# Linear attention, a dense MLP and a Sinkhorn mixture of experts in one kernel: every engine takes its instructions in the order of the source

## The chip, the cores and the metric

The kernel runs on one core of a Trainium2 chip. The engines named below are TensorE (PE, with its weight loads PEld), VectorE (DVE), ScalarE (ACT), GpSimd (POOL) and SyncE (SP, which issues the DMAs). The metric is the device time of one execution in microseconds (us), as the median of several runs.

## The reference

Three layers follow each other. The input of the first is q, k, v of 4 x 8 x 576 x 64; the two others work on 2304 tokens of 512 features, all in float32.

```python
# linear attention: softmax of q over its features, of k over the sequence
kv = np.einsum('bhsd,bhse->bhde', k_s, v)
x = np.einsum('bhsd,bhde->bhse', q_s, kv)          # -> 2304 x 512
# dense MLP, d_ff 2048
h = x @ w_in
x = np.maximum(0.01 * h, h) @ w_out
# mixture of 8 experts (512 -> 1024 -> 512), gates balanced by Sinkhorn
P = np.exp(x @ w_gate - (x @ w_gate).max())
for _ in range(8):
    P /= P.sum(1, keepdims=True) + 1e-09
    P /= P.sum(0, keepdims=True) + 1e-09
    P *= N / E
for e in range(E):
    out += P[:, e:e + 1] * (np.maximum(x @ w1[e], 0.0) @ w2[e])
```

## The kernel before

**Precision.** A float32 operand is split in two parts, hi (a rounded cast, on ACT) and lo (the remainder, on DVE or POOL), and each product is three matmuls: hi times hi, hi times lo, lo times hi.

**The dense MLP** runs in 96 steps: four phases of weights, in each six blocks of 384 tokens, in each four weight units. `first(s)` (twelve matmuls into a tile `ph`) gives the hidden tile: ACT writes `hh` hi and `g`, DVE writes `hh` lo from them (L188 to L190). `second(s)` (twelve matmuls into `y0` to `y3`) adds the hidden tile's share to the output, which at the end of four units goes to `acc` (L209 on ACT in phase 0, L211 on DVE later). A step is issued as two half-steps, and `first` runs one or two steps ahead of `second`.

**What is laid around the steps.** A table of half-steps (`at`, `plan`, `half_step`) says where other work is issued: `k_task` and `q_task` (attention of the next blocks, in phase 0), `prep_half(u, half)` (the conversion of half a weight unit: ACT L134, DVE L136, L137, L140, ACT L144, DVE L145, L146, POOL L148, L149, then the DMA of another half), the gates (`pg`) and, in phase 3, the first pairs of expert weights. Units 4 to 7 (phase 1) are converted at half-steps 35 to 47, units 8 to 11 from half-step 51 on and units 12 to 15 from 99 on, one half every 4.5 half-steps.

**The mixture** runs in 96 groups, 32 for each superblock of 768 tokens. `group(i)` has seven half-steps: t0 to t3 hold seven products of six matmuls (banks `pa` to `pd`; sums `c1`, `c2` on DVE, their hidden values in `xs`), t4 to t6 three output tiles `e` of twelve matmuls for the pair of groups before. Beside them a group converts the next group's weights: `wa<-pair`, `wa<-s` and `wb_t<-pair` (ACT L397, DVE L398), and DVE adds each `e` to `acc` (L491). `pre` is empty in groups 0 and 1, so the source has no `e` there. `balance` (the Sinkhorn iterations, matmuls `pmx`, `pmb`, `pcs0` to `pcs7`) is issued from group 0 on. `x_sums(sb)` makes the seven sums B11 to T4 of a superblock's input (four subtractions at L429, seven splits at L397/L398 into `xs`); for the second and third superblock it is issued from half-step t3 of groups 31 and 63, one piece per half-step.

**Who sets the order.** The source is written to the tile framework, which inserts the semaphores. Before the change its scheduler also orders each engine's instructions: by readiness and priority, so that an instruction whose inputs are there can be put ahead of others written earlier. An engine works through its own list from top to bottom.

## Time and profile before

| what | value |
|---|---|
| median of 3 runs | 2077.51 us (2077.18 to 2080.61) |
| the profiled execution | 2077.42 us, of which 2075.6 us lie in the span from the first to the last instruction |
| busy over the span | PE 98%, DVE 63%, ACT 38%, POOL 24% |
| mean granted clock of PE | 0.987 |
| the chain that ended last | PE 86%, DVE 6%, issue 5%, ACT 1%, DMA 1%, POOL 1% |

The shares are means over stages with different limits. The span falls into the dense MLP with the attention (0 to 554.8 us), the head of the mixture with the Sinkhorn iterations (554.8 to 619.4 us), and the rest of the mixture. In the windows PE busy below the window's length is time that PE stood still, and a PEclk below 1.00 is time at the lower of two clock levels.

### The profile page before, as it was taken

To read this page: it belongs to the slowest core of one execution; us is meant where nothing else is said; L and a number is where in the kernel's file an instruction comes from. 1 tells how busy PE (TensorE), PEld (TensorE's weight loads), DVE (VectorE), ACT (ScalarE), POOL (GpSimd) and SP (SyncE) were. 2 spreads that over 40 slices of the span, in tenths; PEclk is the share of its full clock that TensorE was granted. 3 is DMA by queue.
4 is the path that set the end of the run, shared out by engine and by line. 5 is a ranking of instruction groups with operands and counts; after the bars stand their busy time and mean duration, and the time that the engine had idled before them with its cause. 6 is when DMAs were issued, how large, how long until landed. Compare 5 with 4: busy or idle time off the path is not lost.

```text
span 2075.6 us, 26519 instructions
## 1 busy us (share of the span) xinstructions
PE 2024.7 (98%) x10447; PEld 1850.2 (89%) x10447; DVE 1303.4 (63%) x1899; ACT 794.1 (38%) x1342; POOL 508.3 (24%) x492
## 2 busy tenths in 40 slices
PE   7898798999999999999999999999999999999999
PEld 6898798999988988988988898898888889889887
DVE  8826826234486666666675666666676666666664
ACT  6644322223343343333344333343344433333431
POOL 5604404001121222222222212212212222222220
PEclk9999899999999999999999999999999999999999
DMA  6402202000121221221221211211213212212210
GB/s 239 151 7 74 89 3 89 1 1 1 42 81 41 82 82 41 82 82 41 82 97 57 81 64 59 82 56 67 82 41 112 81 41 81 82 41 82 82 41 31
DMA packets 65453, 138.57 MB, mean 67 GB/s; under 512 B 4656, under 2 KB 4656, under 8 KB 65328
## 3 DMA queue, kind: packets, MB, share of 16 engines
q1 hardware_dynamic: 65328, 136.87, 19.3%
q8 instruction: 82, 1.34, 0.3%
q14 instruction: 43, 0.35, 0.0%
HBM read 132.14 MB, written 4.72 MB: 66 GB/s over the span
## 4 chain that ended last, share of the span: by engine, by line
PE 86%; DVE 6%; issue 5%; ACT 1%; DMA 1%; POOL 1%; SPq 0%; POOLq 0%; ACTq 0%; DVEq 0%
PE e L172 38%; PE pa L172 9%; PE pc L172 9%; PE pd L172 9%; PE y L172 7%; PE ph L172 6%; PE pb L172 5%; DVE ca L140 1%; DVE ca L136 1%; DVE hh L190 1%; PE pg L172 1%; PE px L172 1%; DVE ca L137 1%; DVE raw L146 1%; PE pkv L172 1%
## 5 line engine op out<-in xcount | busy, mean ns | idle before, releaser
L172 PE MATMUL e<-wb_t,xs 128*128 128x512 f32 x3456 | 823.0, 395 | 0.2 <-DVE xs L498 0.2
L172 PEld LDWEIGHTS e<-wb_t,xs 128*128 128x128 f32 x3456 | 647.0, 188 | 149.6 <-DVE xs L498 0.7
L404 POOL TENSOR_TENSOR s<-pair 128x256 f32<-128x256 f32 x96 | 74.3, 774 | 1276.3 <-DMA pair<-in_w 703.8
L491 DVE SCALAR_TENSOR_TENSOR acc<-e,pm,acc 128x512 f32<-128x512 f32 x264 | 193.3, 745 | 104.9 <-PE e L172 102.3
L498 DVE SCALAR_TENSOR_TENSOR xs<-c,xs 128x384 fp32r<-128x384 f32 (+1 forms) x192 | 185.0, 982 | 84.2 <-ACT xs L497 81.1
L172 PE MATMUL pa<-xs,wa 128*128 128x384 f32 x1152 | 231.3, 335 | 2.2 <-ACT c L523 2.2
L172 PE MATMUL pc<-xs,wa 128*128 128x384 f32 x1152 | 230.8, 334 | 0.0
L172 PE MATMUL pd<-xs,wa 128*128 128x384 f32 x1152 | 230.6, 334 | 0.0
L497 ACT ACTIVATE xs<-c 128x768 fp32r<-128x768 f32 x192 | 126.6, 681 | 235.3 <-PE e L172 214.7
L172 PEld LDWEIGHTS pa<-xs,wa 128*128 128x128 f32 x1152 | 203.4, 188 | 11.5 <-ACT c L523 3.1
L172 PEld LDWEIGHTS pd<-xs,wa 128*128 128x128 f32 x1152 | 202.4, 188 | 0.0
L172 PEld LDWEIGHTS pc<-xs,wa 128*128 128x128 f32 x1152 | 202.3, 188 | 0.0
L190 DVE TENSOR_TENSOR hh<-g,hh 128x384 fp32r<-128x384 f32 x96 | 68.3, 712 | 187.6 <-ACT g L189 187.5
L398 DVE TENSOR_TENSOR wa<-s,wa 128x768 fp32r<-128x768 f32 x96 | 91.9, 957 | 105.0 <-ACT wa L397 102.8
L397 ACT CAST wa<-s 128x768 fp32r<-128x768 f32 x96 | 80.1, 835 | 174.4 <-POOL s L407 150.6
L513 DVE TENSOR_TENSOR c<-c 128x384 f32<-128x384 f32 x96 | 53.9, 562 | 135.3 <-ACT c L533 135.3
L172 PE MATMUL y<-hh,wa 128*128 128x384 f32 x576 | 119.8, 358 | 15.8 <-DVE acc L211 5.4
L172 PE MATMUL y<-hh,wb_t 128*128 128x384 f32 x576 | 118.6, 356 | 13.8 <-DVE hh L190 5.1
L523 ACT COPY c<-pa 128x384 f32<-128x384 f32 x96 | 46.2, 481 | 215.5 <-PE pa L172 164.9
L172 PEld LDWEIGHTS y<-hh,wa 128*128 128x128 f32 x576 | 108.0, 200 | 18.7 <-DVE hh L190 6.2
L172 PEld LDWEIGHTS y<-hh,wb_t 128*128 128x128 f32 x576 | 108.4, 202 | 16.6 <-DVE hh L190 6.4
L398 DVE TENSOR_TENSOR wa<-pair,wa 128x1024 fp32r<-128x1024 f32 x96 | 119.6, 1246 | 3.2 <-PE y L172 2.8
(106 smaller groups left out, 2515.5 us busy)
## 6 DMA issues: line engine op xcount, KB each, us to landing
pair<-in_w SPq DMA_DIRECT2D x192, 512.0 KB, 4.9
raw<-in_wm SPq DMA_DIRECT2D x32, 512.0 KB, 3.8
v<-in_vt SPq DMA_DIRECT2D x16, 320.0 KB, 4.7
k<-in_kt SPq DMA_DIRECT2D x16, 288.0 KB, 4.2
out<-acc SPq DMA_DIRECT2D x18, 256.0 KB, 2.0
acc<-in_q SPq DMA_DIRECT2D x5, 768.0 KB, 5.9
acc<-in_q SPq DMA_DIRECT2D x3, 256.0 KB, 5.2
wg_t<-in_wg SPq DMA_DIRECT2D x1, 16.0 KB, 8.9
```

What stands on the lines that cost most here:

```text
L136: nc.vector.tensor_scalar(af, af, EXP_MIN, EXP_MAX, op0=ALU.max, op1=ALU.min)
L137: nc.vector.tensor_scalar(a, a, 3, 0x3FFFFFFF, op0=ALU.logical_shift_left, op1=ALU.bitwise_and)
L172: nc.tensor.matmul(o, a, b, start=start, stop=stop, **more)
L190: nc.vector.tensor_tensor(hh[:, 1, :], g, r32(hh[:, 0, :]), op=ALU.subtract)
L397: nc.scalar.copy(hi, a)
L398: return lambda: nc.vector.tensor_tensor(lo, a, r32(hi), op=ALU.subtract)
L404: nc.gpsimd.tensor_tensor(s[:, 0], a21, a22, op=ALU.add)
L491: nc.vector.scalar_tensor_tensor(a, y, scale, a, op0=ALU.mult, op1=ALU.add)
L497: nc.scalar.activation(o[:, 0], p, AF.Relu)
L498: nc.vector.scalar_tensor_tensor(o[:, 1], p, 0.0, r32(o[:, 0]), op0=ALU.max, op1=ALU.subtract)
L513: add = lambda o, x, y: nc.vector.tensor_tensor(o, x, y, op=ALU.add)
L523: nc.scalar.copy(c1, bk[0])
```

## The change

The kernel enters a manual schedule: every engine's list is the order in which the source issues the instructions. With it the temporary `t1` of `x_sums` takes another buffer for the second and third superblock: tag `hh` of the pool `h` (two buffers, shared with `hh` and `c2`) in place of tag `s` (one buffer, shared with the sums of `pair_sums`).

```diff
@@ -68,6 +68,8 @@
     US = 4 * DM
     HX = KC // 2 * BLK
 
+
+    ctx.enter_context(tc.manual_schedule())
     const = ctx.enter_context(tc.tile_pool(name="const", bufs=1))
@@ -423,7 +425,8 @@
         b11, b12, b21, b22 = b
-        t1 = later["mo"].tile([P, KC // 2, BLK], F32, tag="s", name=f"t1_{sb}", bufs=1)
+        pool, tag, bufs = (hp_, "hh", 2) if sb else (later["mo"], "s", 1)
+        t1 = pool.tile([P, KC // 2, BLK], F32, tag=tag, name=f"t1_{sb}", bufs=bufs)
```

No instruction of the computation is added or taken away; lists change. Line numbers of the kernel after are higher by 2, and by 3 behind the second edit. Three places follow.

VectorE in phase 0, around steps 24 to 27 (`hhN` is the lo part of step N's hidden tile; `caU_H` and `rawU_H` are the conversion of half H of unit U; units 8 and 9 are needed in phase 2, from step 48 on). Before:

```order
L190 TENSOR_TENSOR hh23_1868<-g23_1869,hh23_1868 128x384
L146 SCALAR_TENSOR_TENSOR raw8_0_1941<-raw8_0_1941 128x512
L136 TENSOR_SCALAR ca9_0_2123<-ca9_0_2123 128x512
L137 TENSOR_SCALAR ca9_0_2123<-ca9_0_2123 128x512
L140 SCALAR_TENSOR_TENSOR ca9_0_2123<-raw9_0_1987,ca9_0_2123 128x512
L145 TENSOR_SCALAR raw9_0_1987<-ca9_0_2123 128x512
L146 SCALAR_TENSOR_TENSOR raw9_0_1987<-raw9_0_1987 128x512
L190 TENSOR_TENSOR hh24_1913<-g24_1914,hh24_1913 128x384
```

After, the same engine, four steps later in the program:

```order
L192 TENSOR_TENSOR hh26_2007<-g26_2008,hh26_2007 128x384
L147 TENSOR_SCALAR raw7_1_1922<-ca7_1_1969 128x512
L148 SCALAR_TENSOR_TENSOR raw7_1_1922<-raw7_1_1922 128x512
L192 TENSOR_TENSOR hh27_2048<-g27_2049,hh27_2048 128x384
L138 TENSOR_SCALAR ca8_0_2053<-ca8_0_2053 128x512
L139 TENSOR_SCALAR ca8_0_2053<-ca8_0_2053 128x512
L142 SCALAR_TENSOR_TENSOR ca8_0_2053<-raw8_0_1943,ca8_0_2053 128x512
L192 TENSOR_TENSOR hh28_2083<-g28_2084,hh28_2083 128x384
L147 TENSOR_SCALAR raw8_0_1943<-ca8_0_2053 128x512
L148 SCALAR_TENSOR_TENSOR raw8_0_1943<-raw8_0_1943 128x512
L192 TENSOR_TENSOR hh29_2120<-g29_2121,hh29_2120 128x384
```

The conversion of unit 8, which stood ahead of `hh24` before, now begins behind `hh27`, and one such half stands between several steps' hidden tiles; that of unit 9 comes later still.

TensorE at the Sinkhorn iterations (`pcsN` is the matmul of iteration N, `pX_1` are products of group 1, `e0_N` output tiles of groups 0 and 1). Before:

```order
L172 MATMUL pcs1_4740<-cs1_4698,ones_71 128x8
L172 MATMUL pd_1_4667<-xs_81,wa_82 128x384 x6
L172 MATMUL e0_0_4891<-wb_t_1680,xs_81 128x512 x2
L172 MATMUL e0_1_4907<-wb_t_1680,xs_81 128x512 x5
L172 MATMUL e0_0_4891<-wb_t_1680,xs_81 128x512 x2
L172 MATMUL e0_1_4907<-wb_t_1680,xs_81 128x512 x2
L172 MATMUL e0_0_4891<-wb_t_1680,xs_81 128x512
L172 MATMUL e0_1_4907<-wb_t_1680,xs_81 128x512 x2
L172 MATMUL e0_2_4935<-wb_t_1680,xs_81 128x512 x11
L172 MATMUL pcs2_4765<-cs2_4747,ones_71 128x8
L172 MATMUL e0_3_5028<-wb_t_1680,xs_81 128x512 x10
L172 MATMUL pcs3_4779<-cs3_4772,ones_71 128x8
```

After:

```order
L326 MATMUL pmx_4649<-ident_72,mrow_93 1x128
L174 MATMUL pmb_4654<-mall_94,ones_73 128x1
L174 MATMUL pa_1_4666<-xs_83,wa_84 128x384 x6
L174 MATMUL pb_1_4667<-xs_83,wa_84 128x384 x6
L174 MATMUL pcs0_4693<-cs0_4660,ones_73 128x8
L174 MATMUL pc_1_4668<-xs_83,wa_84 128x384 x6
L174 MATMUL pd_1_4669<-xs_83,wa_84 128x384 x6
L174 MATMUL pa_1_4666<-xs_83,wa_84 128x384 x6
L174 MATMUL pc_1_4668<-xs_83,wa_84 128x384 x6
L174 MATMUL pcs1_4742<-cs1_4700,ones_73 128x8
L174 MATMUL pd_1_4669<-xs_83,wa_84 128x384 x6
L174 MATMUL pcs2_4767<-cs2_4749,ones_73 128x8
```

The `e0` matmuls that stood between `pcs1`, `pcs2` and `pcs3` are gone from here (they now start in group 2, behind `pcs5`), and so are those between `pmx` and `pmb`; the next row after is `pcs3`.

VectorE at the boundary of superblocks in group 31 (`t1_1`, `acc2`, `acc3` belong to `x_sums(1)`, `xs` from them are its splits, `wa<-pair32` and `wa<-s32` the weights of the next group, L429 and L398 of before are L432 and L400 after). Before:

```order
L429 TENSOR_TENSOR t1_1_8328<-acc3_78,acc2_77 128x768
L398 TENSOR_TENSOR wa_82<-pair32_8207,wa_82 128x1024
L491 SCALAR_TENSOR_TENSOR acc0_75<-e14_1_8236,pm_74,acc0_75 128x512
L429 TENSOR_TENSOR acc3_78<-acc3_78 128x768
L491 SCALAR_TENSOR_TENSOR acc0_75<-e14_2_8251,pm_74,acc0_75 128x512
L513 TENSOR_TENSOR c1_31_8270<-pb_31_8266,c1_31_8270 128x384
L398 TENSOR_TENSOR xs_81<-acc2_77,xs_81 128x768
L398 TENSOR_TENSOR xs_81<-t1_1_8328,xs_81 128x768
L513 TENSOR_TENSOR c2_31_8269<-c2_31_8269 128x384
L398 TENSOR_TENSOR xs_81<-acc3_78,xs_81 128x768
L513 TENSOR_TENSOR c2_31_8269<-c2_31_8269,c1_31_8270 128x384
L498 SCALAR_TENSOR_TENSOR xs_81<-pa_31_8265,xs_81 128x384
```

After:

```order
L432 TENSOR_TENSOR t1_1_8330<-acc3_80,acc2_79 128x768
L432 TENSOR_TENSOR acc3_80<-acc3_80 128x768
L516 TENSOR_TENSOR c1_31_8272<-pd_31_8270,c1_31_8272 128x384
L501 SCALAR_TENSOR_TENSOR xs_83<-c1_31_8272,xs_83 128x384
L400 TENSOR_TENSOR xs_83<-acc2_79,xs_83 128x768
L400 TENSOR_TENSOR xs_83<-acc3_80,xs_83 128x768
L494 SCALAR_TENSOR_TENSOR acc1_78<-e14_3_8347,pm_76,acc1_78 128x512
L400 TENSOR_TENSOR wa_84<-pair32_8209,wa_84 128x1024
L432 TENSOR_TENSOR acc3_80<-acc3_80,t1_1_8330 128x768
L400 TENSOR_TENSOR xs_83<-acc3_80,xs_83 128x768
L400 TENSOR_TENSOR xs_83<-t1_1_8330,xs_83 128x768
L494 SCALAR_TENSOR_TENSOR acc1_78<-e14_4_8368,pm_76,acc1_78 128x512
```

Before, the subtractions and splits stand between the sums of group 31 from its first product on, and `wa<-s32` stands ahead of `t1_1`. After, all of `x_sums` stands behind those sums, with `wa<-pair32` behind two of its splits and `wa<-s32` behind four.

## Rows read from the trace of the kernel before

**Rows 1.** The page, part 1: busy us (share of the span) and instructions of TensorE.

```profile
PE 2024.7 (98%) x10447; PEld 1850.2 (89%) x10447; DVE 1303.4 (63%) x1899; ACT 794.1 (38%) x1342; POOL 508.3 (24%) x492
```

**Rows 2.** Windows: from:to length, PE busy (matmuls), PEld, DVE, ACT, POOL busy, PEclk.

```profile
62.00:89.00 27.00, 22.13 (x125) 20.88 (x125) 22.82 (x57) 19.48 (x43) 18.64 (x17) 0.88 0.52 182
...
180.00:248.00 68.00, 50.13 (x229) 47.09 (x228) 66.78 (x83) 27.38 (x55) 39.52 (x26) 0.86 0.35 109
248.00:307.00 59.00, 59.00 (x335) 59.00 (x334) 19.46 (x38) 13.55 (x30) 0.19 (x1) 0.99 0.00 1
...
554.80:619.40 64.60, 61.95 (x332) 55.20 (x331) 53.92 (x117) 29.24 (x48) 17.95 (x16) 1.00 0.22 73
```

**Rows 3.** Timeline of PE around steps 18 to 29: start us, us, [idle before].

```profile
182.57 2.27 PE L172 MATMUL ph<-xs,wa 128*128 128x384 f32 x12
...
249.25 0.94 PE L172 MATMUL ph<-xs,wb_t 128*128 128x384 f32 x4
```

**Rows 4.** Timeline of PE where units 13 to 15 are converted: two step starts.

```profile
320.80 2.25 PE L172 MATMUL ph<-xs,wa 128*128 128x384 f32 x12
...
342.07 1.21 PE L172 MATMUL ph<-xs,wa 128*128 128x384 f32 x6
```

**Rows 5.** Lines by form, first 620 us: xcount | busy us, mean ns | idle before.

```profile
L146 DVE SCALAR_TENSOR_TENSOR raw<-raw 128x512 f32<-128x512 uint32 x32 | 33.7, 1054 | 0.4
L140 DVE SCALAR_TENSOR_TENSOR ca<-raw,ca 128x512 uint32<-128x512 uint32 x32 | 29.0, 905 | 0.4
...
L136 DVE TENSOR_SCALAR ca<-ca 128x512 f32<-128x512 f32 x32 | 23.2, 724 | 6.7 <-ACT ca L134 6.6
...
L137 DVE TENSOR_SCALAR ca<-ca 128x512 uint32<-128x512 uint32 x32 | 21.9, 684 | 0.4
...
L145 DVE TENSOR_SCALAR raw<-ca 128x512 uint32<-128x512 uint32 x32 | 18.1, 566 | 0.4
...
L271 DVE TENSOR_REDUCE qmx<-acc 128x8 f32<-128x512 f32 x18 | 12.0, 669 | 0.2 <-DMA acc<-in_q 0.2
L237 DVE TENSOR_REDUCE knm<-k 128x1 f32<-128x576 f32 x16 | 11.9, 746 | 5.8 <-DMA k<-in_kt 5.6
```

**Rows 6.** Timeline of DVE: the same L146 row at two moments.

```profile
187.49 1.77 DVE L146 SCALAR_TENSOR_TENSOR raw<-raw 128x512 f32<-128x512 uint32 x1
...
217.46 0.69 DVE L146 SCALAR_TENSOR_TENSOR raw<-raw 128x512 f32<-128x512 uint32 x1
```

**Rows 7.** Timeline of PE, steps 4 to 7 of phase 0.

```profile
76.69 2.20 PE L172 MATMUL y<-hh,wa 128*128 128x384 f32 x11 [1.34 <-DVE hh L190]
...
86.30 1.08 PE L285 MATMUL pq<-ident,acc 128*128 128x128 f32 x4 [2.48 <-ACT g L189]
...
88.75 4.00 PE L172 MATMUL y<-hh,wa 128*128 128x384 f32 x12
...
106.68 2.28 PE L172 MATMUL y<-hh,wa 128*128 128x384 f32 x12
```

**Rows 8.** Timeline of DVE: the second Sinkhorn iteration's first and last row ahead of its matmul.

```profile
572.22 0.30 DVE L336 TENSOR_REDUCE rs<-pm 128x18 f32<-128x144 f32 x1
...
573.41 0.42 DVE L340 TENSOR_REDUCE cs<-pm 128x8 f32<-128x144 f32 x1
```

**Rows 9.** Chain of waits around group 31: the y tiles at its two ends.

```profile
1040.60 8.40 PE e L172 x36
...
1057.51 4.67 PE e L172 x20
```

**Rows 10.** Windows: one undisturbed group of the mixture.

```profile
648.60:664.28 15.68, 15.68 (x80) 14.04 (x79) 9.97 (x14) 5.84 (x10) 6.53 (x7) 1.00 0.14 52
```

**Rows 11.** Lines by form, 640 to 1030 us: rows of the mixture's groups.

```profile
L491 DVE SCALAR_TENSOR_TENSOR acc<-e,pm,acc 128x512 f32<-128x512 f32 x72 | 52.6, 744 | 25.4 <-PE e L172 24.6
...
L398 DVE TENSOR_TENSOR wa<-pair,wa 128x1024 fp32r<-128x1024 f32 x24 | 29.1, 1212 | 0.0
...
L398 DVE TENSOR_TENSOR wa<-s,wa 128x768 fp32r<-128x768 f32 x25 | 24.0, 958 | 30.6 <-ACT wa L397 30.6
```

## The prediction

> **What bounds the kernel now.** I read the page first, then windows over the first 620 us, the timelines of PE and DVE where PE stands still, and last the groups of the mixture. TensorE is busy 2024.7 of 2075.6 us [rows 1], so over the whole span an order can give back at most about 51 us of standstill, and beside it what the lower clock costs. The windows say where these lie. From 248 to 307 us PE stands nowhere: 335 matmuls in 59 us, 2.11 us for twelve, which is the price of `first` or `second` with nothing in the way. From 62 to 89 us it works 22.13 of 27 us at a clock of 0.88, and from 180 to 248 us 50.13 of 68 us at 0.86, with DVE busy 66.78 of the 68 [rows 2]. The second is the worst stretch of the kernel: VectorE is the bound there, not TensorE. In the mixture one undisturbed group of 80 matmuls takes 15.68 us with PE busy throughout and DVE busy 9.97 [rows 10]; nothing can be won in it. So the change is worth something only in the first 555 us, and the Sinkhorn stretch and the superblock boundaries can only pay.
>
> **The change part by part.** The order of PE's matmuls in the dense MLP is nearly the same in both lists; what differs is what DVE, ACT and POOL put ahead of `hh`, for which `second` waits.
>
> *Conversions of units 8 to 15.* Before, the scheduler starts them as soon as their buffers are free, so eleven halves pile up between `hh20` and `hh28`. One half costs DVE 0.72 + 0.68 + 0.91 + 0.57 + 1.05 = 3.93 us as a mean [rows 5], and a step of 4.23 us also needs its `hh`. From the `ph` at 182.57 to the end of the ninth step after it, where the `ph` at 249.25 begins, 66.7 us pass [rows 3]; nine steps at 2 x 2.115 are 38.1, so 28.6 us are lost. From 320.80 to 342.07, three steps, 21.3 us pass [rows 4] where 12.7 would do: 8.6 us lost. In the list after, units 4 to 7 stand in half-steps 35 to 47, about two halves for three steps, 3.93 x 2 + 3 x 0.71 for the `hh` = 10 us of DVE in 12.7 us, and units 8 to 15 one half in 4.5 half-steps, 3.93 in 9.5 us. Both fit. I put the return at 36 of the 37.2 us, with 32 as the lower end, since the stretch at 35 to 47 holds up to five DVE rows of a half ahead of one `hh` and a late `hh` there costs up to 1 to 2 us in each of two or three steps.
>
> *The first eight steps.* Here PE waits for DVE too: 22.82 of 27 us busy [rows 2]. Before `hh4` the list before holds 12 maxima of k (L237) and 12 of q (L271), the list after 8 and 9: 4 x 0.746 + 3 x 0.669 = 5.0 us less [rows 5]; three q sums (L277, of the same width, so 2.0 us) leave as well, and a dozen and a half of small rows behind the sums, for some 8 us in all. Before `hh8` three conversions, four k and six q maxima and nine q sums leave, over 20 us. I move the end of step 4's `y`, which begins its last eleven matmuls at 76.69 [rows 7], up by 8 us. Behind it PE needs the same work as before to the `y` of step 7 (from 106.68), but it stood 2.48 us at 86.30, and the twelve matmuls at 88.75 took 4.00 in place of 2.11 at the lower clock [rows 7]: 4.4 us that DVE no longer causes, and some 0.7 in the transposes between them. Together 13 us. Against it, `ph0` starts later: the lo part of the third x tile stands behind three rows of a conversion, one k and two q maxima, 0.72 + 0.68 + 0.91 + 0.75 + 2 x 0.67 = 4.4 us [rows 5]. That is the same DVE work in another order, so I count it only as the lower end: 13 - 4.4 - 3.6 for in-order waits = 5 us; the upper end is 15. I take 12.
>
> *Steps 8 to 17* hold the last attention tasks and are bound by PE; in strict order a task's ACT copy can stand behind a cast that waits. Zero to 6 us lost; I take 2.
>
> The first part sums to 36 + 12 - 2 = 46 us gained, so the mixture begins near 509 us rather than at 554.8.
>
> *The Sinkhorn stretch.* Before, PE stands only 64.60 - 61.95 = 2.65 us in it [rows 2], because 82 `e0` matmuls are put between the iterations. They are gone from there after, so PE follows DVE. Four gaps arise. Between group 0's last product and `pa_1` lie the last sum and hidden part of group 0 on DVE (two rows of 384 elements, about 1.2 us with the crossing into each) and the split of `wa<-pair1` (1.21 us [rows 11]), with a cast of the same width on ACT partly ahead of it: 3.1 to 4.3 us. Ahead of `pcs2` stand one iteration and a split: from the first to the last row ahead of its matmul an iteration takes 573.41 + 0.42 - 572.22 = 1.61 us [rows 8], the three rows behind the matmul about half of that, the split 1.21, less the 1.04 us of `pd_1` on PE: with the crossings between engines 3.6 us. Ahead of `pcs3`, which follows at once, stand `c1_1`, its hidden part (1.2), another split (1.21) and a whole iteration (2.4), with the crossings 5.5 us. One short gap of 0.4 follows. That is 12.6 to 13.8 us, less 2.65: 10 to 11. Counted at equal work at the end of group 4 I get 9.2 without a fall of the clock. I take 10, with 8.5 and 12 as ends.
> The Trainium skill ("PSUM — Partial Sum Buffer", section "Engine vs sequencer instructions") says that the queues of VectorE, ScalarE and GpSimd are strictly first in, first out and that matmuls start in program order. It speaks against this change here: no ready `e0` can pass a waiting `pcs3`. If an engine did look ahead, this term would be about zero and the sum 10 us lower; no row of before tests it.
>
> *The two superblock boundaries.* Before, the stretch from one group's `e` at 1040.60 to the next at 1057.51 is 16.91 us [rows 9] against 15.68 [rows 10]: 1.2 us for each. After, four subtractions and seven splits of 128 x 768 (0.96 each, the row of that shape [rows 11]) stand in DVE's list behind the last product of group 31 and ahead of `c1_32`, with two weight splits (1.21 + 0.96 [rows 11]), three `acc` additions (0.74 each [rows 11]) and the last sum and hidden parts of group 31 (two rows of 384 elements and one of 768: about 2 by the row of 768): 10.5 + 2.2 + 2.2 + 2 = 17 us. The three `e` tiles give 8.4 us of cover [rows 9] and the first two products of group 32 another 2.1. That leaves at least 6.5 us, and up to 9.5 if ACT's copy of `pa_32`, which stands behind its last cast, and the crossings add their own. I take 8 for each: 16 less 2.4, 13.6 us lost for both.
>
> *The 92 undisturbed groups.* In the list after, the next group's `wa` splits end some 3 us ahead of their use, and PE's 15.68 us are full [rows 10]. I count nothing. The price if that is wrong: 0.1 us in each group is 9 us.
>
> *The t1 buffer, the DMAs, the tail.* `t1` in its new buffer only keeps the boundary's first subtraction from waiting for `s`; its cost is in the boundary. SP's list keeps each load behind the work that frees its buffer, as before, and the mixture's loads keep two groups of distance. Nothing.
>
> Sum, from the profiled 2077.4 us (0.1 below the median): 2077.4 - 46 + 10 + 13.6 = 2055; with a part of the steady groups' risk, 2056.
>
> **A page's rule on the conversions.** The same row L146 takes 1.77 us at one moment and 0.69 at another [rows 6], in the same stretch of the kernel. The Trainium skill ("SBUF — State Buffer", section "SBUF: two separate sides") has it that a VectorE operation with two SBUF inputs and a GpSimd operation shut each other out of a shared port pair. By it, conversions that meet POOL less often would be cheaper. Rows alone say: if all five rows fell as L146 falls from its mean, by 0.69 / 1.05, a half would cost 2.6 us and the eight halves ahead of `hh8` 10 us less. POOL is busy 18.64 of 27 us there [rows 2], so I keep 3.93; the cheap reading is the second rival.
>
> **The rivals.**
> *Slower: a steady group grows.* Strict order may let one late row (a cast on ACT behind a hidden part, an `acc` addition ahead of a sum) delay `pa` in every group. For it: three engines feed each group and 92 semaphore waits are added on PE. Against: DVE is busy 9.97 of 15.68 [rows 10]. It decides from (46 - 23.6) / 92 = 0.24 us a group on; at 0.4 us the time is 2056 + 37 = 2093.
> *Larger gain.* The spread conversions run at their undisturbed price, the first steps return 20 rather than 12 us, and the boundary costs 5 rather than 8 each: 2056 - 8 - 6 = 2042, or 2034 if ready work fills the Sinkhorn gaps better too.
> *The first part gains little.* In-order waits on ACT and POOL take the place of the piled conversions, so that of 46 us only 15 to 30 come back: 2071 to 2086. For it: in phase 0 DVE, ACT and POOL are each busy two thirds or more of the time [rows 2], and each change of order between them can make another wait. Against: the sums above leave room.
> *Nothing changes.* PE's list is nearly the same, so the waits could be too: 2077. The loss of 28.6 us hangs on DVE's list, which differs, so this is small.
>
> **How the numbers follow.** A difference of 0.2% (4.2 us) is about what a measurement of this kernel can tell. My forecast, 2046 to 2070, has 0.58; the larger gain 0.14; the first part gaining little 0.14, of which 0.04 lie below 2073.3, 0.05 within 0.2% and 0.05 above; a growing group 0.11; nothing 0.03. Faster: 0.58 + 0.14 + 0.04 = 0.76. Same: 0.05 + 0.03 = 0.08. Slower: 0.05 + 0.11 = 0.16. The range for 8 in 10 leaves one tenth at each side: the low end in the larger gain, 2036, the high end in the rivals that cost, 2085; the likeliest case alone spans 2046 (52 gained, 9 and 12 paid) to 2070 (40 gained, 12 and 17 paid, and the rest of the groups' risk).
>
> **What would show it.** After, the window of steps 18 to 29 has PE busy nearly throughout and its steps at 4.23 us; `y` of step 7 ends near 97; `pa_0` starts near 509; PE shows gaps of 3 to 6 us ahead of `pa_1`, `pcs2` and `pcs3`; groups 31 and 63 are followed by a stretch of about 23 us where 15.68 is usual; other groups stay at 15.68. It is wrong if a usual group is over 15.8 us, if DVE's `hh` rows still hold PE in steps 18 to 29, or if the boundaries stay near 17.

## The result, and the profile after

The kernel became slower: 2104.74 us as the median of three executions (2103.51 to 2107.41) against 2078.03 (2077.18 to 2080.61, four), a ratio of 1.0123 with an interval of 1.0107 to 1.0138. A fourth execution, at a granted clock of 0.555 over its whole span, took 3321.54 us and is left out. Forecast were 2056 us, with 2036 to 2085 as the range; the time lies 20 us above its upper end.

The profiled execution took 2107.41 us, its span 2105.6: 30.0 us more than before. The page's part 1, busy us and share of the span of each engine, answers to [rows 1]:

```profile
PE 2037.3 (97%) x10447; PEld 1858.0 (88%) x10447; DVE 1282.9 (61%) x1899; ACT 772.9 (37%) x1342; POOL 473.6 (22%) x492
```

PE now stands still for 68 us, 17 more than before, and it is also busy 12.6 us longer for the same 10447 matmuls. That is the lower clock: busy time by mean granted clock is 2037.3 x 0.980 = 1997 us, and was 2024.7 x 0.987 = 1998. The others work less than before: VectorE by 20 us, GpSimd by 35. Nothing has more to do; the same work waits more. The windows tell where (from:to length, PE busy, PEld, DVE, ACT, POOL, PEclk, DMA share, GB/s):

```profile
180.00:250.00 70.00, 61.08 (x327) 59.85 (x326) 49.12 (x73) 26.84 (x57) 33.59 (x22) 0.93 0.25 76
250.00:307.00 57.00, 54.42 (x308) 53.55 (x307) 26.50 (x52) 16.46 (x35) 15.74 (x11) 1.00 0.19 56
...
490.00:555.40 65.40, 60.67 (x327) 59.07 (x327) 23.68 (x36) 14.04 (x30) 4.98 (x4) 0.90 0.00 1
555.40:632.00 76.60, 64.87 (x332) 58.95 (x331) 54.61 (x119) 29.36 (x49) 12.26 (x16) 0.91 0.16 56
```

The worst stretch of before is better: from 180 us PE is busy 61.08 of 70 us, where it was 50.13 of 68 [rows 2], and DVE, which was full, is idle for 21 us of it, though not where PE waits (see the conversions). But from 250 us, where PE stood nowhere, it now stands for 2.6 us; at the end of the dense MLP (490 to 555.4) for 4.7 us at a clock of 0.90; and in the Sinkhorn stretch for 11.7 us where 2.65 were lost.

Set side by side, the starts of the same tiles on PE in the two traces give the account. Each entry is the change of the time between two starts, so the rows add up:

| stretch | predicted gain, us | measured gain, us |
|---|---|---|
| to `ph` of step 7 | 12 | 1.4 |
| steps 7 to 22 | -2 (steps 8 to 17) | -3.0 |
| steps 22 to 31 (units 4 to 9) | 36 with the next but one | 16.2 |
| steps 31 to 48 | 0 | -3.5 |
| steps 48 to 51 (units 13 to 15) | in the 36 | 8.5 |
| step 51 to `pa_0` | 0 | -21.1 |
| group 0 to group 8 (Sinkhorn) | -10 | -12.4 |
| group 32, group 64 | -13.6 together | -7.2 and -8.8 |
| the other groups | 0 | 0.0 |
| sum (of the unrounded) | 22.4 | -30.0 |

In sum the mixture came near the forecast, 28.4 us lost where 23.6 were priced. The head is what failed: 46 us were to come back, 26.0 did, and 27.6 were lost elsewhere in it; `pa_0` begins at 555.55 us, 1.6 later than before.

A stretch of one execution is not exact. Three kernels below (`bal16`, `bal_we`, `xs_early`) issue the same up to `pa_0`, which comes 3.4 to 3.9 us later than before in them, and in seven kernels that leave groups 0 to 8 as they are this stretch loses 12.4 to 14.3 us. A difference of 2 us in one row of one run thus decides nothing.

### The profile page after: what moved, and what is told of

Read it like the earlier page. It is cut to its first block, busy times and chain, and to the rows that moved or that the text cites. A ratio compares the mean times of both kernels' runs of the same rounds, so it can differ in the third digit from the quotient of the medians.

```text
span 2105.6 us, 26340 instructions
## 1 busy us (share of the span) xinstructions
PE 2037.3 (97%) x10447; PEld 1858.0 (88%) x10447; DVE 1282.9 (61%) x1899; ACT 772.9 (37%) x1342; POOL 473.6 (22%) x492
## 4 chain that ended last, share of the span: by engine, by line
PE 90%; DVE 7%; ACT 2%; issue 1%; DMA 0%; POOL 0%; SPq 0%; ACTq 0%
PE e L174 38%; PE y L174 9%; PE pa L174 9%; PE pc L174 9%; PE pd L174 9%; PE ph L174 8%; PE pb L174 5%; DVE xs L400 1%; DVE ca L138 1%; PE pg L174 1%; PE px L174 1%; PE pkv L174 1%; DVE ca L139 1%; DVE acc L213 1%; DVE hh L192 0%
## 5 line engine op out<-in xcount | busy, mean ns | idle before, releaser
L494 DVE SCALAR_TENSOR_TENSOR acc<-e,pm,acc 128x512 f32<-128x512 f32 x264 | 198.3, 751 | 213.2 <-PE e L174 213.0
L500 ACT ACTIVATE xs<-c 128x384 fp32r<-128x384 f32 x192 | 131.5, 685 | 402.6 <-DVE c L516 267.0
L501 DVE SCALAR_TENSOR_TENSOR xs<-c,xs 128x384 fp32r<-128x384 f32 x192 | 174.2, 907 | 80.1 <-ACT xs L500 80.1
L192 DVE TENSOR_TENSOR hh<-g,hh 128x384 fp32r<-128x384 f32 x96 | 56.2, 585 | 243.4 <-ACT g L191 243.3
L190 ACT ACTIVATE hh<-ph 128x384 fp32r<-128x384 f32 x96 | 47.0, 490 | 260.0 <-PE y L174 244.4
L174 PE MATMUL pb<-xs,wa 128*128 128x384 f32 x576 | 119.3, 341 | 6.5 <-DVE wa L400 3.9
L409 POOL TENSOR_TENSOR s<-pair,s 128x256 f32<-128x256 f32 x96 | 123.2, 1283 | 7.5
L174 PE MATMUL ph<-xs,wa 128*128 128x384 f32 x576 | 113.6, 346 | 6.9 <-DVE xs L303 5.5
L400 DVE TENSOR_TENSOR wa<-pair,wa 128x1024 fp32r<-128x1024 f32 x96 | 116.7, 1215 | 2.9 <-ACT wa L399 2.9
```

The lines of the kernel that those rows point to most:

```text
L174: nc.tensor.matmul(o, a, b, start=start, stop=stop, **more)
L190: nc.scalar.activation(hh[:, 0, :], p, AF.Prelu, alpha=0.01)
L192: nc.vector.tensor_tensor(hh[:, 1, :], g, r32(hh[:, 0, :]), op=ALU.subtract)
L400: return lambda: nc.vector.tensor_tensor(lo, a, r32(hi), op=ALU.subtract)
L409: nc.gpsimd.tensor_tensor(s[:, 2], a12, s[:, 1], op=ALU.subtract)
L494: nc.vector.scalar_tensor_tensor(a, y, scale, a, op0=ALU.mult, op1=ALU.add)
```

## The experiments

Each kernel is the one after with the edit shown, if nothing else is said; "start" is the first matmul of a tile on PE. Runs without an interval are one execution; kernels tried together ran on one chip, beside the kernel before.

### The mixture alone

`mix_only` enters the manual schedule just ahead of the loop over groups, so that the head keeps the scheduler's order.

```diff
-    ctx.enter_context(tc.manual_schedule())      # at the top
+    ctx.enter_context(tc.manual_schedule())      # ahead of: t = END
     t = END
```

> The scheduler orders the first 555 us as before; only the mixture is in source order, with the new buffer of t1. Main theory: the mixture's own lists cost 28.4 us (Sinkhorn stretch 12.4, boundaries 7.2 and 8.8), whatever comes ahead of it: pa_0 within 2 us of 554, total 2104 to 2108. Rival: part of that loss is handed over by the dense MLP's order (late weights, late first sums): total under 2097.

It took 2108.93 us beside 2080.12 before. `pa_0` begins 1.5 us later than before, `pa_8` 15.5, `pa_33` 22.7, `pa_65` 31.5: the mixture in source order costs 30.0 us here, 28.4 behind the manual head, and that head as it stands is worth nothing.

### Where the head's gain went: the ends of blocks

A block of 384 tokens ends every four steps with DVE's `acc` additions. In the source `first(s+2)` is written a half-step ahead of `second(s)`, so on every engine the hidden part of step s+2 stands ahead of the `acc` rows of step s. Timelines of the kernel after around such an end (start us, us, engine, line, operation, out<-in, count, [idle before]); first PE, then ACT, then DVE:

```profile
439.12 2.25 PE L174 MATMUL y<-hh,wb_t 128*128 128x384 f32 x12
...
443.44 4.39 PE L174 MATMUL pg<-wg_t,acc 128*128 128x8 f32 x24
```

```profile
441.41 0.49 ACT L190 ACTIVATE hh<-ph 128x384 fp32r<-128x384 f32 x1 [3.34 <-PE y L174]
```

```profile
442.31 0.56 DVE L192 TENSOR_TENSOR hh<-g,hh 128x384 fp32r<-128x384 f32 x1 [3.65 <-ACT g L191]
442.79 1.94 DVE L213 TENSOR_TENSOR acc<-y,acc 128x384 f32<-128x384 f32 x4
```

ACT's `hh` waits 3.34 us for the `y` on PE: there are two `hh` buffers, and this one is still read. DVE's `hh` waits 3.65 us for ACT, and the four `acc` rows wait behind it. They begin 3.67 us after `y` does. The same place before, DVE and then PE:

```profile
454.75 2.12 DVE L211 TENSOR_TENSOR acc<-y,acc 128x384 f32<-128x384 f32 x4 [1.18 <-PE y L172]
...
457.64 0.55 DVE L190 TENSOR_TENSOR hh<-g,hh 128x384 fp32r<-128x384 f32 x1
```

```profile
454.02 2.25 PE L172 MATMUL y<-hh,wb_t 128*128 128x384 f32 x12
...
458.23 2.74 PE L172 MATMUL pg<-wg_t,acc 128*128 128x8 f32 x24
```

There `acc` begins 0.73 us after `y`, beside it, and the gate's matmuls `pg` are done in 2.74 us, not in 4.39. The row at the end of the last block but one shows the wait on PE itself, ahead of a `pg` at the lower clock:

```profile
537.18 5.31 PE L174 MATMUL pg<-wg_t,acc 128*128 128x8 f32 x24 [4.32 <-DVE acc L213]
```

`accf` leaves the matmuls of `first` where they are and moves only its three hidden rows (ACT and DVE) behind `second` of the same half-step pair, from the step on where `first` runs two steps ahead.

```diff
+        if s - 1 < FAR:
+            hidden(s, p)
+        else:
+            tails.append((s, p))
...
-        half_step(2 * s + 1, second, s)
+        half_step(2 * s + 1, lambda: [second(s)] + [hidden(*tails.pop(0)) for _ in tails[:]])
```

> Source order; from step 13 on the hidden part of a step that runs two ahead (ScalarE's hh and g, VectorE's lo) is issued behind second(s) and not ahead of it. New theory: at a block's end the rows into acc stand behind hh of step s + 2, and that hh waits for the buffer which y of step s still reads, so the acc rows start after y has ended and not beside it; gates and the next block's y wait. With it gone the loss from step 51 to pa_0 falls from 21 us to 6 or less, total 2089 to 2096. Rival: gates and block ends cost this by the clock or by the conversions, whatever stands ahead of acc: loss still over 15, total 2100 or more.

It took 2083.40 us. `pa_0` begins at 531.54, 24.0 us earlier than after: 2.9 us in steps 17 to 22, 2.0 in steps 22 to 31, 3.6 in steps 31 to 48, and 15.3 from step 51 to `pa_0`. Steps 31 to 48 and 51 to 75 now take what they took before, 4.21 and 4.23 us each. DVE and PE at a block's end:

```profile
426.60 2.12 DVE L221 TENSOR_TENSOR acc<-y,acc 128x384 f32<-128x384 f32 x4 [1.18 <-PE y L174]
...
429.06 0.56 DVE L200 TENSOR_TENSOR hh<-g,hh 128x384 fp32r<-128x384 f32 x1 [0.35 <-ACT g L199]
```

```profile
430.07 2.74 PE L174 MATMUL pg<-wg_t,acc 128*128 128x8 f32 x24
```

The picture of before is back, and `all4` and `all5` below, with the same edit, begin `pa_0` 23.0 and 22.0 us earlier than before. So the loss at the ends of blocks hangs on the place of three rows in two lists, not on the manual order as such. Some 6 us stay lost in steps 91 to 95; there a row of `x_sums` still stands ahead of the `acc` rows on DVE.

Of the 15.3 us, 4.5 come back in steps 51 to 75, at a granted clock of 1.00 in both runs: this is the wait alone. But 8.3 come back in steps 75 to 91, where PE hardly stands still even in the kernel after (windows from the start of `ph75` to that of `ph91`, after and then before):

```profile
428.59:517.96 89.37, 88.67 (x481) 86.47 (x481) 18.47 (x34) 15.84 (x37) 0.00 (x0) 0.90 0.00 1
```

```profile
443.49:526.13 82.64, 82.64 (x482) 82.64 (x481) 30.14 (x45) 22.01 (x45) 5.31 (x4) 0.94 0.00 1
```

PE stands for 0.70 us and is busy 6.0 us longer, at the lower clock. This part varies: `bal16`, `bal_we`, `xs_early` and `q2_early`, whose lists are the same in these steps, lose 9.9, 9.0, 9.0 and 0.5 us here against before. The six kernels with the edit of `accf` lose nothing here or gain up to 1.6. The direction is thus shown, the size of this part isn't.

### The conversions: why only 24.6 us of 37.2 came back

Over steps 22 to 31 as a whole DVE is no longer full. PE waits here:

```profile
205.16 2.29 PE L174 MATMUL ph<-xs,wb_t 128*128 128x384 f32 x12
...
214.05 3.77 PE L174 MATMUL y<-hh,wb_t 128*128 128x384 f32 x12 [6.60 <-ACT acc L211]
```

```profile
212.44 0.62 ACT L146 CAST wb_t<-ca 128x512 fp32r<-128x512 f32 x1 [3.16 <-DVE ca L142]
212.97 0.66 ACT L136 ACTIVATE ca<-raw 128x512 f32<-128x512 f32 x1
213.53 1.60 ACT L211 COPY acc<-y 128x384 f32<-128x384 f32 x4
```

How full the engines are in the 15 us up to that `y`, the window tells (columns as above):

```profile
199.00:214.05 15.05, 8.45 (x49) 8.13 (x48) 14.60 (x19) 5.70 (x13) 8.68 (x7) 0.88 0.33 97
```

Before the `y` at 214.05 PE stands 6.60 us for the `acc` copies on ACT, which empty the `y` banks. They stand in ACT's list behind a cast that waited 3.16 us for DVE, and behind the next half's first row. DVE has no time left here: it is busy for 14.60 of the 15.05 us, with conversion halves one behind the other. Its idle time lies elsewhere in the stretch. (The Trainium skill, "PSUM — Partial Sum Buffer", section "Engine vs sequencer instructions", says that ScalarE's queue is strictly first in, first out; these rows agree.) `late` lets a half's rows be issued behind the `first` or `second` of their half-step, where the kernel issues them ahead.

```diff
+        late = [x for x in active if x[1] == LATE]    # prep_half of units 4 to 15, x_sums(0)
         now = [x for x in active if x[1] not in (PE_NEXT, LATE)]
...
         advance(reversed(then))
+        advance(late)
```

> Source order, but the conversions of units 4 to 15 and the first x_sums are issued behind the step's own instructions in each half-step, not ahead of them. Main theory: the dense MLP loses its gain at the ends of blocks, where the copies or additions into acc stand behind a conversion or a split; from step 51 to the mixture that is 21 us, and some 9 us in steps 18 to 27: total 2106 - 12 to 18 = 2088 to 2094, each block end without a gate under 0.5 us late. Rival: the block ends wait for DVE's backlog and not for the place in the list: total 2102 or more.

2104.38 us, so the main theory failed: the block ends behind step 51 hardly change by it. `ph27` comes 2.7 us earlier than after, `ph31` 2.0 and `pa_0` 3.3. From step 22 to 31 that is 1.5 us; the copies behind the cast don't account for the 12.4 that are missing there.

`no_pool` moves the last two rows of a conversion from GpSimd to DVE.

```diff
-        nc.gpsimd.tensor_tensor(af, af, r32(hi), op=ALU.subtract)
-        nc.gpsimd.tensor_tensor(lo, af, ef, op=ALU.add)
+        nc.vector.tensor_tensor(af, af, r32(hi), op=ALU.subtract)
+        nc.vector.tensor_tensor(lo, af, ef, op=ALU.add)
```

> Source order, with the two GpSimd rows of a conversion done on VectorE. Main theory: in source order the two first rows of each half meet GpSimd's rows of the half before and take 1.4 to 1.5 us in place of 0.42, so a half costs VectorE 4.7 us; without GpSimd it is 2.6 + 2 x 0.7 = 4.0 and ScalarE's cast no longer waits for it: steps 18 to 27 give back 5 to 10 us and the first eight steps some: total 2092 to 2101. Rival: VectorE is the bound there and gets two rows more: total 2106 to 2118.

2104.15 us; `ph26` comes 2.6 us earlier than after, `ph31` 1.0, `pa_0` 4.9. Of these, 4.7 arise between steps 75 and 91, where no unit is converted and where the clock varies as shown above, so they can't be put down to this edit. The groups of DVE's rows from 175 to 240 us (xcount | busy us, mean ns | idle before), after and then in this run, answer to [rows 5]:

```profile
L138 DVE TENSOR_SCALAR ca<-ca 128x512 f32<-128x512 f32 x10 | 11.9, 1190 | 0.0
L139 DVE TENSOR_SCALAR ca<-ca 128x512 uint32<-128x512 uint32 x10 | 8.2, 824 | 0.3
```

```profile
L139 DVE TENSOR_SCALAR ca<-ca 128x512 uint32<-128x512 uint32 x10 | 4.3, 428 | 0.3
...
L138 DVE TENSOR_SCALAR ca<-ca 128x512 f32<-128x512 f32 x10 | 4.2, 420 | 0.0
```

With GpSimd's rows away L138 falls from 1.19 to 0.42 us and L139 from 0.82 to 0.43. So GpSimd does stretch DVE, by 1.2 us a half; but the two rows that it gave up take 1.4 us on DVE (0.68 and 0.69), and a half costs DVE about as much. PE's loss in steps 22 to 31 falls by 2.0 of 12.4 us only, as one would expect where DVE's work is the limit.

### The front

The first two products, `ph0` and `ph1`, end 10.3 us later than before, at 44.18 in place of 33.92 us, where I had priced 4.4. (The start of `ph1` would say 12.7, but before its first matmul stood ahead of the second of `ph0`.) PE before, then after:

```profile
28.86 5.06 PE L172 MATMUL ph<-xs,wa 128*128 128x384 f32 x22
```

```profile
31.29 0.69 PE L174 MATMUL ph<-xs,wa 128*128 128x384 f32 x1 [0.68 <-ACT xs L302]
37.22 6.96 PE L174 MATMUL ph<-xs,wa 128*128 128x384 f32 x23 [5.24 <-DVE xs L303]
```

`q2_early` lets the third q task of the first block begin one half-step earlier, so that its x tile's rows stand ahead of a conversion's.

```diff
-    for j, t in enumerate((0, 2, 3)):
+    for j, t in enumerate((0, 2, 2)):
```

> Source order, with the third q task one half-step earlier, so that the lo part of the third x tile stands ahead of the rows of conversion 2_0, one k and two q maxima in VectorE's list. Theory: the first two products wait 12.7 us longer than before since these rows stand ahead of that lo part; in the trace of source order they take 1.49 + 1.38 + 0.69 + 0.75 + 1.27 us, with two rows of conversion 0_1 (1.1) 6.7 us. The matmuls of step 1 come 5 to 7 us earlier, ph7 3 to 6 us: total 2100 to 2103. Rival: VectorE is the bound there in any order, so hh0 or a later row is late by as much: ph7 within 1.5 us of the changed kernel's 94.5, total 2104 or more.

2105.94 us. The two products end 6.7 us earlier, at 37.51, but the next rows on PE wait instead, at 43.72 (2.88 us for `hh`) and here:

```profile
60.79 0.78 PE L249 MATMUL pk<-ident,k 128*128 128x128 f32 x5 [3.51 <-ACT g L191]
```

`ph7` comes 4.2 us later than after. `pa_0` comes 1.4 earlier, but steps 75 to 91, whose lists are the same, give more than that by their clock. In the rows of the front PE waits for DVE, for ACT and (at 55.24 us, 0.56) for POOL in turn: a row moved ahead in one list puts another behind. Which order would be best there stays open.

### The Sinkhorn stretch

The kernel after, on PE, with the waits that were forecast:

```profile
568.46 0.38 PE L174 MATMUL pmb<-mall,ones 1*128 1x1 f32 x2 [2.67 <-DVE mall L327]
...
582.20 0.44 PE L174 MATMUL pcs<-cs,ones 128*128 128x8 f32 x2 [3.05 <-DVE cs L342]
...
587.71 0.59 PE L174 MATMUL pcs<-cs,ones 128*128 128x8 f32 x2 [5.07 <-DVE cs L342]
588.16 2.27 PE L174 MATMUL pa<-xs,wa 128*128 128x384 f32 x6
```

`bal16` issues the iterations two groups later, where there are `e` matmuls to stand between them.

```diff
-    at(END + 2, balance)
+    at(END + 16, balance)
```

> Source order, with the Sinkhorn task issued 14 half-steps later, from group 2 on, where output tiles stand between its matmuls. Main theory: the 12.4 us of that stretch are the lack of other matmuls between the iterations; 8 to 10 us come back (the wait ahead of group 1 for its weights stays): total 2095 to 2099. Rival: VectorE's list is too full for the iterations wherever they stand: total 2103 or more, with waits for cs at the new place.

2106.32 us: the stretch from `pa_0` to `pa_8` lost 9.5 in place of 12.4 us. The waits for `cs` are gone, but ahead of groups 1 and 2 PE waits for weights:

```profile
570.45 0.85 PE L174 MATMUL pa<-xs,wa 128*128 128x384 f32 x2 [2.93 <-ACT wa L399]
...
582.91 0.61 PE L174 MATMUL pa<-xs,wa 128*128 128x384 f32 x2 [2.93 <-ACT wa L399]
```

Groups 0 and 1 have no `e` in the source, so their products take 7.3 us, and the next group's splits, written for a group of 15.68 us, come too late. `bal_we` adds to `bal16` that groups 0 and 1 split the next group's weights at t1 and t2 and not at t3 to t5.

```diff
-            if nxt:
+            if nxt and i > 1:
                 rest.append(pair_w1(i + 1, 0))
...
+            if i < 2:                       # end of t1; at the end of t2 pair_w1(i + 1, 1)
+                pair_w1(i + 1, 0)()
```

> Source order; the Sinkhorn task 14 half-steps later, and the expert weights of groups 1 and 2 converted two half-steps earlier, in t1 and t2 of the group before. Theory after the run with the late Sinkhorn task alone: there the two waits of 3.3 and 3.6 us ahead of groups 1 and 2, for their weights, took the place of the waits for the iterations, since groups 0 and 1 have no output tiles that cover a conversion. Both edits together: loss from pa_0 to pa_8 against the kernel before 3 us or less in place of 12.4, total 2094 to 2099. Rival: in the products' half-steps the conversions delay the sums, and the loss stays over 8.

2104.99 us; 7.9 us lost, where the expectation was 3 or less (7.2 in `all4` and 5.5 in `all5`, with the same edits here). PE still waits for the weights of groups 1 and 2, now mostly for the second part:

```profile
572.62 0.96 PE L174 MATMUL pb<-xs,wa 128*128 128x384 f32 x4 [1.62 <-DVE wa L400]
...
583.71 1.65 PE L174 MATMUL pb<-xs,wa 128*128 128x384 f32 x4 [1.59 <-DVE wa L400]
```

Most of the term thus stays when the iterations are moved away. I put it down to the missing `e` matmuls, since the first two groups have 14.6 us of products on PE and a whole group's conversions each on DVE and ACT; no run has `e` matmuls there in source order, so this is argued, not shown.

### The boundaries of superblocks

PE, DVE and ACT after, around the start of group 32:

```profile
1063.75 0.97 PE L174 MATMUL pa<-xs,wa 128*128 128x384 f32 x4 [0.43 <-DVE wa L400]
...
1068.87 1.65 PE L174 MATMUL pb<-xs,wa 128*128 128x384 f32 x4 [1.96 <-DVE wa L400]
...
1075.27 1.33 PE L174 MATMUL pa<-xs,wa 128*128 128x384 f32 x6 [1.05 <-ACT c L526]
```

```profile
1060.08 1.83 DVE L400 TENSOR_TENSOR xs<-acc,xs 128x768 fp32r<-128x768 f32 x2 [1.11 <-ACT xs L399]
...
1067.87 0.95 DVE L400 TENSOR_TENSOR wa<-s,wa 128x768 fp32r<-128x768 f32 x1
```

```profile
1073.28 0.83 ACT L399 CAST xs<-acc 128x768 fp32r<-128x768 f32 x1 [5.65 <-DVE acc L432]
...
1074.76 0.46 ACT L526 COPY c<-pa 128x384 f32<-128x384 f32 x1
```

The last of these fences is ACT: its copy of `pa`, for which PE waits at 1075.27, stands behind the last cast of the sums. The split of `wa<-s32`, which `pb` needs, stands behind the splits of `x_sums`, as the order showed. `xs_early` starts `x_sums` two half-steps earlier, in other pieces.

```diff
-            at(t + 3, x_sums, i // NQ + 1)
+            at(t + 1, x_sums, i // NQ + 1)
```

> Source order; x_sums of the second and third superblock begins two half-steps earlier (t1 of groups 31 and 63), and takes its seven parts in the order B11, T1, T3, B22, B21, T2, T4 in which group 31's products free their places. Main theory: the boundaries cost 7.2 and 8.8 us because all of x_sums stands in VectorE's list between group 31's last product and group 32's first sum; spread over t1 to t5 each costs 1 to 3: total 2092 to 2097. Rival: the rows only move the wait into group 31: total 2102 or more.

2113.97 us, and the boundaries lose 9.3 and 9.2 us, more than the 7.2 and 8.8 of after. The weights became later still: in this list `wa<-pair32` stands behind six of the seven splits and `wa<-s32` behind all seven, where it was two and four.

```profile
1071.65 1.63 PE L174 MATMUL pa<-xs,wa 128*128 128x384 f32 x4 [4.25 <-DVE wa L400]
...
1075.96 1.65 PE L174 MATMUL pb<-xs,wa 128*128 128x384 f32 x4 [2.03 <-DVE wa L400]
```

`all4` puts `accf`, `xs_early` and `bal_we` together; its edits are those shown.

> Source order with the three edits together: hidden parts behind second, x_sums early, Sinkhorn late with early weights. If the causes are separate, the savings add: 2106 - 13 - 12 - 9 = 2072, range 2064 to 2080, below or near the kernel before. If they share a cause (the clock at the gates, VectorE's total work), less than two thirds of it, 2083 or more.

2078.53 us (2076.05 to 2080.43), a ratio of 0.9989 (0.9979 to 0.9998) to the kernel before: the loss of the change is taken back, and little more. `pa_0` is 23.0 us early, of which the Sinkhorn stretch loses 7.2 and the boundaries 8.4 and 8.7.

`all5` is `accf` and `bal_we`, with the weights of groups 32 and 64 split at t1 and t2 as well, and `x_sums` begun at t6 of groups 30 and 62, in other pieces again, so that `wa<-pair32` stands behind one of its splits and `wa<-s32` behind three. The diff is against `bal_we`.

```diff
+        early = i < 2 or i % NQ == NQ - 1
...
-            if i < 2:
+            if nxt and early:
                 pair_w1(i + 1, 0)()
...
-        if i % NQ == NQ - 1 and i < NG - 1:
-            at(t + 3, x_sums, i // NQ + 1)
+        if i % NQ == NQ - 2 and i < NG - 2:
+            at(t + 6, x_sums, i // NQ + 1)
```

> Source order for everything with the hidden parts behind second, the late Sinkhorn task, early weights, and a new boundary: x_sums begins in the last half-step of group 30 (62), and the weights of group 32 (64) are converted in t1 and t2 ahead of it. Theory: the earlier start alone did not help since the weight splits for the next group still stood behind x_sums' subtractions and splits, each of which waits for a cast on ScalarE and the casts for VectorE; with the weights ahead, each boundary costs 1 to 4 us in place of 9: total 2076.8 - 10 to 16 = 2061 to 2067. Rival: VectorE's work in the two groups is the bound: each boundary still over 6 us, total 2072 or more.

2065.88 us (2063.24 to 2066.7), a ratio of 0.9925 (0.9909 to 0.9942). The boundaries lose 2.7 and 3.1 us now, and the Sinkhorn stretch 5.5. Two things differ from `xs_early`: the sums begin two half-steps earlier still, and the weights stand ahead of most splits. Since an earlier start alone had cost time, I put the gain down to the weights; no run has them alone.

### The other edit, and the best of both orders

`t1_alone` is the kernel before with the new buffer for `t1` alone.

```diff
-        t1 = later["mo"].tile([P, KC // 2, BLK], F32, tag="s", name=f"t1_{sb}", bufs=1)
+        pool, tag, bufs = (hp_, "hh", 2) if sb else (later["mo"], "s", 1)
+        t1 = pool.tile([P, KC // 2, BLK], F32, tag=tag, name=f"t1_{sb}", bufs=bufs)
```

> The kernel before with the new buffer of t1 alone, the scheduler's order kept. Main theory: the buffer costs and gives nothing by itself, the boundaries stay at 16.9 us and the total within 2 us of the kernel before. Rival: part of the boundaries' 16 us is the buffer (t1 waits for c2's place): total 2080 to 2094, with longer boundaries.

2077.30 us beside 2080.45 (2077.58 to 2082.12). The times alone wouldn't tell, but in the trace each boundary is 1.2 us shorter, 2.4 together: all that [rows 9] had over [rows 10].

`head_accf` is `accf` with the manual schedule closed ahead of the loop over groups, so that the scheduler orders the mixture.

```diff
+    head = ctx.enter_context(ExitStack())
+    head.enter_context(tc.manual_schedule())
...
+    head.close()
     t = END
```

> Source order for the dense MLP alone, with the hidden parts behind second; from the mixture on the scheduler orders as before. Main theory: the dense MLP gives 22.4 us (measured as pa_0 at 531.5), and the mixture costs what it does before, 1521.6 us: total 2055, range 2052 to 2060, clearly faster than before. Rival: the scheduler's mixture needs what its own order of the head had done early, and loses 10 us or more of it: 2065 or more.

2056.64 us (2055.78 to 2057.72), a ratio of 0.9885 (0.9871 to 0.99). `pa_0` is 20.2 us early, and nothing of it is given back: `pa_65` is 21.1 early.

`head2` adds `late`, the halves of units 4 to 7 at half-steps 35, 37, ... 49, and the first `x_sums` six half-steps later.

```diff
-zip((35, 36, 38, 40, 42, 43, 45, 47), halves)
+zip((35, 37, 39, 41, 43, 45, 47, 49), halves)
...
-    at(T3 + 34, x_sums, 0)
+    at(T3 + 40, x_sums, 0)
```

> As the run before, and the conversions of units 4 to 15 behind the step's own rows, those of units 4 to 7 every other half-step from 35 to 49, and the first x_sums six half-steps later. Theory: what is left of the dense MLP's loss in steps 18 to 95 is ScalarE's copies into acc behind a cast that waits for VectorE (the step of 13.6 us at step 26) and the additions behind x_sums' splits at step 91 (6 us); 8 to 14 us more come back: total 2042 to 2048. Rival: VectorE's 5 us for a half are the bound in half-steps 35 to 55 however they are laid, and only the 6 us come back, or none if units 4 to 7 arrive late: 2049 or more.

2053.99 us (2049.58 to 2060.15), a ratio of 0.9874 (0.985 to 0.9899), the fastest here, though its interval overlaps that of `head_accf`. From `ph91` to `ph95` nothing is lost, where `accf` lost 6.3, and steps 22 to 31 return 20.8 us. But part of the wait at the end has only moved: `pa_0` is 34.5 us early and `pa_1` 24.9, since ahead of the last block's gate PE now stands for `acc`. That row, and behind it what is left in steps 22 to 31, a wait for the weights themselves:

```profile
530.08 0.60 PE L175 MATMUL pg<-wg_t,acc 128*128 128x8 f32 x2 [4.85 <-DVE acc L222]
```

```profile
204.75 0.62 PE L175 MATMUL ph<-xs,wb_t 128*128 128x384 f32 x2 [1.85 <-ACT wb_t L147]
...
208.20 3.57 PE L175 MATMUL ph<-xs,wb_t 128*128 128x384 f32 x10 [2.83 <-POOL wb_t L152]
```

`head3` adds the edit of `q2_early` to `head2`; no line is new.

> The fastest version so far (source order for the dense MLP alone, hidden parts behind second, conversions behind the step, a later first x_sums; the scheduler's order in the mixture) with the third q task one half-step earlier. If the front's gain stays: 2054 - 3 to 6 = 2048 to 2051; if VectorE gives it back: 2052 to 2056. Clearly faster than before either way.

2055.85 us (2052.19 to 2059.61), a ratio of 0.9876 (0.9857 to 0.9895): no better than `head2`. The front's gain of 6 us at `ph1` is gone at `ph7`, which comes 2.2 us later than in `head2`.

## Why the prediction was wrong, point by point

**The step that failed** is the sum of the dense MLP: 46 us gained, so that the mixture would begin near 509 us. It rested on the sentence that the order of PE's matmuls is nearly the same and that only what stands ahead of `hh` differs. I followed the rows ahead of `hh` on DVE and never those behind it. At each block's end the rows behind it are `acc`, and `hh` itself waits for the `y` that frees its buffer. `accf`, which moves the three hidden rows alone, begins `pa_0` 24.0 us earlier. This mechanism stands in none of the terms: steps 31 to 48 and step 51 to `pa_0` were put at nothing without a reason, and lost 3.5 and 21.1 us, the second in part by PE's waits and in part by the lower clock in the last blocks. The rival "the first part gains little" named waits on ACT and POOL in general and was the nearest, but at the ends of its range 15 to 30 us still came back, where 1.6 were lost.

**Conversions of units 8 to 15: 36 predicted, 24.6 measured** (16.2 and 8.5, rounded). The direction was right, and the three steps of [rows 4] came back whole (8.5 of 8.6). In steps 22 to 31 "both fit" was wrong by a miscount: the eight halves of units 4 to 7 begin within twelve half-steps, about two for three half-steps, not for three steps. With the `hh` of six and a half steps they are 8 x 3.93 + 6.5 x 0.71 = 36 us of DVE in 27.5. VectorE was still the limit there, as before, only for a shorter time: where PE lost 6.60 us DVE was busy for 14.60 of 15.05. `accf` returns 2.0 us here and `late` 1.5; `head2`, with both and with the halves one step apart, returns 20.8 of the 28.6 in all. Even so a step has 3.93 + 0.71 = 4.6 us of DVE in 4.23. The other 8 us I haven't taken apart.

**The first eight steps: 12 predicted, 1.4 measured.** From the end of the first two products to `ph7` 11.6 us came back, near the 13 priced; but those products end 10.3 us later, not 4.4. I added up the durations of the rows put ahead of one split, as if they had nothing to wait for. I also put the 2.48 us wait of [rows 7] down to DVE, where the row names ACT's `g`. `q2_early` shows that 6.7 of the 10.3 us hang on where one q task begins, and that they can't be had by moving that task alone; the rest isn't taken apart.

**Steps 8 to 17: 2 lost predicted, 3.0 measured** between steps 7 and 22, all of it behind step 17, and gone in `accf`: the block's end, not the attention.

**The Sinkhorn stretch: 10 predicted, 12.4 measured.** The mechanism was right, with gaps of 2.67, 3.05 and 5.07 us where 3.1 to 4.3 (ahead of `pa_1`; the gap came at `pmb`, one row ahead), 3.6 (`pcs2`) and 5.5 (`pcs3`) were forecast. The gaps are thus no longer than priced: PE stands for 11.73 us of that window in place of 2.65, 9.1 more. The excess is the clock, which I had left out: the window's 332 matmuls take 64.87 us at a clock of 0.91 in place of 61.95 at 1.00, 2.9 more. PE takes nothing from behind a waiting `pcs`, as the forecast had it. What was missed is that most of the term isn't the iterations' own: without them in these groups 9.5 us are still lost (`bal16`).

**The boundaries: 13.6 predicted, 16.0 measured.** The waits are those forecast: `pb` waits for `wa<-s32` behind the sums' splits, and `pa` of the second round for ACT's copy behind its last cast. That the sum is near is luck in part. From `pa_32` to `pa_33` and from `pa_64` to `pa_65` together PE stands 8.4 us longer than before, less than priced, and is busy 39.6 us in place of 31.9, at clocks of 0.86 and 0.87; the clock had no term here either. The 17 us of DVE work are the same in `all5`, which loses 2.7 and 3.1: the work set no floor, its order did.

**The undisturbed groups: 0 predicted, 0.0 measured**, 15.68 us each in both traces. The rival by which each group grows fell.

**The t1 buffer: nothing predicted, 2.4 us gained** in the scheduler's order by `t1_alone`.

**The cheap reading of a conversion** came true in small part: over the head L148 takes 0.78 us after, where it took 1.05 [rows 5], but L138 takes 0.89 where it took 0.72. The five rows of a half come to 3.52 us in place of 3.93; the cheap reading had 2.6.

## What to carry to other kernels

When the source's order takes the place of a scheduler's, look on each engine for a row that waits for a buffer and read what stands behind it: the price is paid there, not at the waiting row. Set a count of busy time against the steps in which the rows stand, not against a longer stretch: VectorE was busy for 49 of 70 us, but for 14.60 of 15.05 us where TensorE waited. And price the clock with each wait: of the 30.0 us lost here, 12.6 are TensorE working longer on the same matmuls. The choice can be made stage by stage: the source's order was worth some 20 us in the dense MLP once three rows had been moved, and cost 28 to 30 in the mixture as written, so that the head in one and the groups in the other beat either alone.

## What the runs showed of the hardware that was not expected

How GpSimd stretches a row of VectorE. Timelines of POOL and then DVE in the kernel after, in one conversion:

```profile
208.26 1.70 POOL L150 TENSOR_TENSOR ca<-ca,wb_t 128x512 f32<-128x512 f32 x1 [1.97 <-DVE raw L147]
210.04 1.36 POOL L151 TENSOR_TENSOR wb_t<-ca,raw 128x512 fp32r<-128x512 f32 x1
```

```profile
208.75 1.49 DVE L138 TENSOR_SCALAR ca<-ca 128x512 f32<-128x512 f32 x1
210.28 1.41 DVE L139 TENSOR_SCALAR ca<-ca 128x512 uint32<-128x512 uint32 x1
211.72 0.69 DVE L142 SCALAR_TENSOR_TENSOR ca<-raw,ca 128x512 uint32<-128x512 uint32 x1
```

Both rows of DVE begin while a row of POOL runs, at 208.26 to 209.96 and at 210.04 to 211.40, and both end 0.28 to 0.29 us behind that row's end, so that most of the 0.42 us that they take alone lies behind it. (The Trainium skill, "SBUF — State Buffer", section "SBUF: two separate sides", has it that whichever of the two begins first holds the shared port pair for its whole instruction; these rows, where GpSimd begins first, agree. By the same section it is not only rows with two inputs that are shut out, as my prediction had quoted it, but those in a two-port mode too. These two read one tile; in which mode they run no trace here shows.)

A wait on PE can cost more than its length. Behind the 4.32 us ahead of the last `pg` but one, 24 matmuls of 128 x 8 took 5.31 us where 2.74 is usual, and behind 5.07 us six of 128 x 384 took 2.27 where 1.20 is: near the ratio of the two clock levels, 1.2 and 2.4 GHz. The mean granted clock of the windows around them was 0.90 and 0.91. But the length of the wait doesn't set that cost: in `accf` the same `pg` took 5.31 us behind a wait of 1.75. And the clock fell without long waits, too: in steps 75 to 91 PE stood 0.70 us in all, at a mean clock of 0.90, and `q2_early`, with the same lists in these steps, had 0.98. What decides between the two the runs don't show.
